# Attention memory term in 64 by 64 TensorE tiles, and the first raw weights in pieces on SyncE's queue

## Chip, cores and metric

The kernel runs on one core of one Trainium2 chip. The metric is the time of one execution in device microseconds, the median over several runs.

## What is computed

Three stages follow each other; each hands its output to the next.

```python
# attention, B=4, H=8, S=576, D=64
scores = q @ k^T / sqrt(D), causal mask, softmax        -> a
local  = a @ v
q_p    = phi(q)                                         # elu(q) + 1
mem    = (q_p @ M_prev) / (q_p @ z_prev + 1e-6)
x      = sigmoid(beta) * mem + (1 - sigmoid(beta)) * local
# feed-forward one: 2304 tokens, 512 -> 2048 -> 512
y      = softplus(x @ w_in) @ w_out
# feed-forward two: 512 -> 1536 -> 512
out    = ((y @ w_a) * (y @ w_b)) @ w_2
```

All inputs and outputs are float32.

## The kernel before

**Attention** works on 16 units, one for each batch and pair of heads (class `Unit`). A unit's q and k lie turned, 64 feature rows of one head in partitions 0 to 63 and those of the other in 64 to 127. `score` (L504) multiplies 64 rows by 128 columns at a time, the two heads beside each other in the two halves of the array's rows. `score_tail` (L531) does the last 64 tokens of both heads with all 128 rows. `memory` (L547) multiplies `ph`, which is phi(q), with `mz`, which holds M_prev and z_prev in 65 columns: for each of five blocks of 128 tokens and each head one float32 matmul with 64 rows and 128 columns of weights (`ph`) and 65 moved columns (`mz`). The trace shows each float32 matmul as two loads of weights and two matmuls. `turn`, `turn_tail` and `spread` (L589, L606, L607, L627) transpose, and `use` and `finish` (L619, L639, L645) multiply with v, 128 rows by 64 columns, into the two halves of the output's partitions.

**The reciprocal sums** of a unit travel through DRAM: DVE copies a transposed row (`rt`, L563), SP writes it to `rsd` (L565) and reads it back into all partitions as `rb` (L568). `finish` multiplies with `rb` on DVE (L635, L647).

**Feed-forward** stages multiply with seven products in place of eight (class `Seven`), each in three passes of rounded and rest parts (L850 for single blocks, L994 for the wide ones). Weights come as raw 64-bit words into two buffers `raw` of 8 KB per partition, and `decode` (L728 to L736) makes float32 of them with DVE and ACT, in halves (step 2) where `left_parts` calls it. The first two blocks of w_in are loaded by ACT's own DMA queue while attention still runs; every later one by SP's. `right_parts` (L775) loads x of a third of the tokens (`raw` from `xs`) for the same stage.

**The order** on all engines is made ahead of time by `Plan.order`: a planner gives every step a duration and a rank (the longest path behind it), plays the engines, and at each moment starts on SP, DVE, ACT and POOL the ready step with the highest rank; PE keeps written order within a stream and takes feed-forward matmuls only where attention has none ready. A DMA of SP takes its place on one modelled lane (`lane`) after the ones before it, and at most `LANES` of them are under way. The order is then fixed: on the chip each queue runs in it, and waits only for data.

Of the kernel before, what the change touches and what calls it, by code (L numbers as in the profile page):

```python
# [12 lines left out]
AF = mybir.ActivationFunctionType  # L13
# [16 lines left out]

FIRST, LAST = (0, 1), (6, 7)
START, CONST, WORDS = 6272, 1280, 55680
SWITCH, LANES = 190, 6


class Step:
# [16 lines left out]
class Plan:  # L53
# [153 lines left out]
    def order(self):  # L207
        steps = self.steps
        for s in steps:
            s.after, s.rank = [], 0  # L210
        for s in steps:
            for d in s.deps:
                steps[d].after.append(s.n)
        for s in reversed(steps):
            far = 0
            for a in s.after:
                t = steps[a]
                far = max(far, t.rank + (0 if t.eng == s.eng == "PE" else s.lag))
            s.rank = s.time + s.size + far
        for s in steps:  # L220
            s.left, s.ready, s.start = len(s.deps), 0.0, None
        engines = ("PE", "DVE", "ACT", "POOL", "SP")
        free = dict.fromkeys(engines, 0.0)
        soon, now = {e: [] for e in engines}, {e: [] for e in engines}
        for s in steps:
            if not s.left:
                heapq.heappush(soon[s.eng], (0.0, s.n))
        t, lane, done, mode, landed, held = 0.0, dict.fromkeys(engines, 0.0), 0, None, [], {"DVE": 0.0, "POOL": 0.0}
        port = None
        while done < len(steps):  # L230
            nxt = float("inf")
            moved = False
            for e in engines:
                while soon[e] and soon[e][0][0] <= t:
                    n = heapq.heappop(soon[e])[1]
                    s = steps[n]
                    heapq.heappush(now[e], ((s.stream, n) if e == "PE" else (-s.rank, n)))
                if free[e] > t:
                    nxt = min(nxt, free[e])
                    continue  # L240
                if e == "SP" and now[e] and len(landed) >= LANES and landed[-LANES] > t:
                    nxt = min(nxt, landed[-LANES])
                    continue
                if not now[e]:
                    if soon[e]:
                        nxt = min(nxt, soon[e][0][0])
                    continue
                s = steps[now[e][0][1]]
                if e in ("DVE", "ACT") and soon[e]:
                    u = max((steps[n] for r, n in soon[e] if r - t < min(0.25 * s.time, 150)), key=lambda u: u.rank, default=None)  # L250
                    if u and u.rank > s.rank + 3000:
                        nxt = min(nxt, u.ready)
                        continue
                if s.port and held[e] > t:
                    free_ = [x for x in now[e] if not steps[x[1]].port]
                    if not free_:
                        nxt = min(nxt, held[e])
                        continue
                    s = steps[min(free_)[1]]
                now[e].remove(next(x for x in now[e] if x[1] == s.n))  # L260
                heapq.heapify(now[e])
                s.start = t
                end = t + s.time
                if s.port:
                    held["POOL" if e == "DVE" else "DVE"] = end
                    if e == "DVE":
                        port = s.n
                    elif port is not None:
                        s.deps.add(port)
                if e == "PE":  # L270
                    if s.mode != mode:
                        end += SWITCH if not mode or s.mode[:2] != mode[:2] else SWITCH // 2 + 30 * (not s.mode[2])
                    mode = s.mode
                free[e] = end
                if s.size:
                    end = lane[e] = max(lane[e], end) + s.size
                    if e == "SP":
                        landed.append(end + s.lag)
                for a in s.after:
                    u = steps[a]  # L280
                    lag = 0 if u.eng == s.eng == "PE" else s.lag
                    u.ready = max(u.ready, end + lag)
                    u.left -= 1
                    if not u.left:
                        heapq.heappush(soon[u.eng], (u.ready, a))
                done += 1
                moved = True
                nxt = min(nxt, free[e])
            if not moved:
                t = nxt  # L290
        self.end = t
        return sorted(steps, key=lambda s: (s.start, s.n))
# [25 lines left out]
def tile_kernel(ctx: ExitStack, tc: tile.TileContext, qt, kt, vt, mz, be, w_in, w_out, w_a, w_b, w_2, out):  # L318
# [111 lines left out]
    both = (top, low)  # L430
# [23 lines left out]
    class Unit:  # L454
# [17 lines left out]
        def prep_k(self, first=False):  # L472
            kr, qr = self.kr, self.qr
            self.qh, self.ql, self.kh, self.kl = (take(n) for n in ("qh", "ql", "kh", "kl"))
            e = V if first else G
            for c, d in ((0, 256), (256, 640)) if first else ((0, 640),):
                k, q = slice(c, min(d, S)), slice(c, d)
                rnd(e, self.kh[:, k], kr[:, k])
                self.begun = {A.activation(out=self.qh[:, q], in_=qr[:, q], func=AF.Copy).n}
                sub(e, self.kl[:, k], kr[:, k], f(self.kh[:, k]))  # L480
                sub(e, self.ql[:, q], qr[:, q], f(self.qh[:, q]))

# [56 lines left out]
        def memory(self, k):  # L539
            p, ph, mz = self.p, self.ph, mzs[self.b % 2]  # L540
            self.mo = mo = blocks(take("mo"))
            nm = take("nm")
            banks = bank[:, k : k + 2]
            s = banks[:, :, 0:325].rearrange("p j (c e) -> p j c e", c=5)
            for c in range(5):
                for j, r in enumerate(both):
                    PE.matmul(  # L547
                        out=s[:, j, c], lhsT=ph[r, 128 * c : 128 * c + 128], rhs=mz[r, p], start=c == 0, stop=True, skip_group_check=True,
                    )
            by = lambda t: t.rearrange("p (j c) -> p j c", j=2)  # L550
            V.scalar_tensor_tensor(out=by(nm), in0=s[:, :, :, 64], scalar=1e-6, in1=by(self.rs), op0=ALU.add, op1=ALU.mult)
            V.reciprocal(out=nm, in_=nm)
            V.tensor_tensor(
                out=mo.rearrange("p c (j e) -> p j c e", j=2), in0=s[:, :, :, 0:64],
                in1=by(nm).unsqueeze(3).to_broadcast([128, 2, 5, 64]), op=ALU.mult,
            )
# [98 lines left out]
    order = [Unit(b, p) for b in range(B) for p in range(NP)]  # L655
# [66 lines left out]

    PASSES = ((0, 0), (0, 1), (1, 0))

    def decode(src, to, step=4, q=SP):

        raw = take("raw").bitcast(U32).rearrange("p (m c) -> p m c", c=2)
        q.dma_start(out=raw, in_=src).deps.update(order[1].begun if q is A else ())  # L728
        four = lambda t: t.rearrange("p (b n) -> p b n", b=4)
        for b in range(0, 4, step):  # L730
            low, high = (four(raw[:, :, i])[:, b : b + step] for i in range(2))
            V.tensor_scalar(out=low, in0=low, scalar1=29, scalar2=None, op0=ALU.logical_shift_right)
            V.scalar_tensor_tensor(out=low, in0=high, scalar=0x80000000, in1=low, op0=ALU.bitwise_and, op1=ALU.bitwise_or)  # L733
            A.activation(out=f(high), in_=f(high), func=AF.Identity, scale=REBIAS)  # L734
            V.tensor_scalar(out=f(high), in0=f(high), scalar1=MOST, scalar2=-MOST, op0=ALU.min, op1=ALU.max)
            V.scalar_tensor_tensor(  # L736
                out=to.bitcast(U32)[:, b : b + step], in0=high, scalar=3, in1=low, op0=ALU.logical_shift_left, op1=ALU.bitwise_or
            )
# [16 lines left out]
    def left_parts(src, at, e=V):  # L755

        w, d = (t.rearrange("p (n h m) -> p n h m", n=7, h=2) for t in twice("w", 3584, at))
        d = d[:, :, 1]
        decode(src, d[:, 0:4], 2, SP if e is V else A)
        left_sums(*(d[:, n] for n in range(7)), e)  # L760
        for n, m in ((0, 1), (1, 2), (4, 5), (2, 4), (5, 7)):
            rnd(A, w[:, n:m, 0], d[:, n:m])
            sub(e, w[:, n:m, 1], d[:, n:m], f(w[:, n:m, 0]))
        return lambda n, h, k: w[:, SLOT[n], h, 128 * k : 128 * k + 128]
# [443 lines left out]
```

## Time and profile before

| | us |
|---|---|
| runs | 938.68, 938.79, 940.41 |
| median | 938.79 |
| profiled execution | 940.39 |
| its span, first to last instruction | 938.6 |
| PE busy in it | 922.6 (98%) |
| DVE, ACT, POOL busy | 791.1 (84%), 566.8 (60%), 103.0 (11%) |
| mean granted TensorE clock | 0.998 |

The profile's times are those of the profiled execution. Attention takes about the first 194 us of the span. In the trace a matmul's shape on the array stands as rows*columns: 64*128 is half of the rows and all columns, 128*64 the reverse. PEld is the weight load that belongs to a matmul.

### The profile page before, as it was taken

Reading aid. Unit: us, or ns where it says so; the run is one execution under the profiler, and the core shown is the slowest. Engines: PE = TensorE matmul, PEld = TensorE weight load, DVE = VectorE, ACT = ScalarE, POOL = GpSimd, SP = SyncE. Lnnn points to the kernel's source line nnn. Section 1 sums busy time; section 2 is a strip of 40 time slices with the busy share of each in tenths; the row PEclk is TensorE's granted clock in tenths of the full one; section 3 lists DMA queues with packets and bytes.
Section 4 is the critical chain, followed back from the end, with each engine's and each line's share of the span. In section 5 each row is a group of like instructions: output and inputs, shape, how many; then the busy total and the mean of one; then the engine's idle time right before and its main releaser. Section 6 shows DMA issues by size and latency. Waiting matters only on the chain.

```text
span 938.6 us, 16918 instructions
## 1 busy us (share of the span) xinstructions
PE 922.6 (98%) x6204; PEld 890.1 (95%) x6204; DVE 791.1 (84%) x1503; ACT 566.8 (60%) x1124; POOL 103.0 (11%) x137
## 2 busy tenths in 40 slices
PE   7989999999999999999999999999999999999998
PEld 6878788899999999999999999999999999999998
DVE  7969989979998946998679999999997566998683
ACT  8968999757766756754446555544444334555452
POOL 6434588200000000000000000000000000000000
PEclk9999999999999999999999999999999999999999
DMA  6654564376988899482641444466654146672701
GB/s 185 193 162 131 169 186 130 99 232 215 312 292 293 267 329 370 172 299 73 202 135 34 134 157 159 159 226 208 224 188 144 43 160 192 245 234 74 225 32 50
DMA packets 81378, 172.10 MB, mean 183 GB/s; under 512 B 7936, under 2 KB 60560, under 8 KB 76048
## 3 DMA queue, kind: packets, MB, share of 16 engines
q1 hardware_dynamic: 80576, 168.61, 54.4%
q10 hardware_dynamic: 720, 2.43, 0.7%
q8 instruction: 48, 0.79, 0.3%
q14 instruction: 34, 0.28, 0.1%
HBM read 110.90 MB, written 60.10 MB: 182 GB/s over the span
## 4 chain that ended last, share of the span: by engine, by line
PE 86%; DVE 5%; ACT 3%; DMA 3%; issue 1%; POOL 1%; SPq 0%; DVEq 0%; POOLq 0%; ACTq 0%
PE bank L850 46%; PE bank L994 33%; DMA rb<-rsd 2%; PE bank L619 1%; PE bank L504 1%; PE bank L589 1%; PE bank L547 1%; DVE eTrue L514 1%; ACT eTrue L518 1%; PE bank L531 1%; ACT eFalse L518 1%; DMA kr<-kt 1%; PE bank L606 1%; PE bank L627 0%; ACT aT L595 0%
## 5 line engine op out<-in xcount | busy, mean ns | idle before, releaser
L340 DVE TENSOR_TENSOR s<-bank,s 128x384 f32<-128x384 f32 x216 | 117.2, 552 | 44.9 <-PE bank L850 38.9
L828 ACT ACTIVATE s<-bank 128x384 f32<-128x384 f32 x72 | 35.1, 487 | 73.2 <-PE bank L850 43.1
L337 DVE TENSOR_TENSOR t<-t,t 128x1536 f32<-128x1536 f32 (+1 forms) x48 | 74.5, 1552 | 0.4
L850 PE MATMUL bank<-x1h,w 128*128 128x384 f32 x240 | 71.0, 335 | 0.0
L850 PE MATMUL bank<-x6h,w 128*128 128x384 f32 x240 | 70.7, 335 | 0.3 <-ACT s L825 0.3
L850 PE MATMUL bank<-x5h,w 128*128 128x384 f32 x240 | 70.5, 334 | 0.0
L850 PE MATMUL bank<-x2h,w 128*128 128x384 f32 x240 | 70.5, 334 | 0.0
L850 PE MATMUL bank<-x3h,w 128*128 128x384 f32 x240 | 70.5, 334 | 0.0
L850 PE MATMUL bank<-x7h,w 128*128 128x384 f32 x240 | 70.5, 334 | 0.0
L850 PE MATMUL bank<-x4h,w 128*128 128x384 f32 x240 | 70.5, 334 | 0.0
L330 ACT ACTIVATE w<-wf 128x256 fp32r<-128x256 f32 (+1 forms) x100 | 50.0, 500 | 20.4 <-DVE w L337 16.4
L886 ACT ACTIVATE s<-s 128x384 f32<-128x384 f32 x72 | 37.2, 523 | 33.0 <-DVE s L340 32.9
L825 ACT ACTIVATE s<-bank 128x384 f32<-128x384 f32 x72 | 35.1, 487 | 35.8 <-PE bank L850 22.9
L330 ACT ACTIVATE gx2h<-t 128x768 fp32r<-128x768 f32 x37 | 31.4, 848 | 35.9 <-PE bank L994 32.7
L337 DVE TENSOR_TENSOR w<-wf,w 128x256 fp32r<-128x256 f32 (+1 forms) x90 | 47.2, 525 | 5.5 <-ACT w L330 4.9
L330 ACT ACTIVATE gx1h<-t 128x768 fp32r<-128x768 f32 x37 | 31.3, 846 | 33.4 <-PE bank L994 33.4
L734 ACT ACTIVATE raw<-raw 128x512 f32<-128x512 f32 (+1 forms) x54 | 42.6, 802 | 12.4 <-DVE raw L733 12.1
L330 ACT ACTIVATE gx0h<-t 128x768 fp32r<-128x768 f32 x37 | 31.3, 846 | 29.4 <-PE bank L994 28.5
L337 DVE TENSOR_TENSOR gx0l<-t,gx0h 128x768 fp32r<-128x768 f32 x37 | 35.3, 954 | 14.2 <-ACT gx0h L330 13.9
L518 ACT ACTIVATE eTrue<-eTrue,mn 128x384 f32<-128x384 f32 (+1 forms) x64 | 42.1, 660 | 8.2 <-DVE mn L514 8.0
L337 DVE TENSOR_TENSOR gx1l<-t,gx1h 128x768 fp32r<-128x768 f32 x37 | 35.3, 954 | 13.2 <-ACT gx1h L330 13.1
L831 ACT ACTIVATE s<-bank 128x384 f32<-128x384 f32 x72 | 35.1, 488 | 18.6 <-PE bank L850 14.6
(344 smaller groups left out, 3040.7 us busy)
## 6 DMA issues: line engine op xcount, KB each, us to landing
gs<-s SPq DMA_DIRECT2D x96, 192.0 KB
t<-gs SPq DMA_DIRECT2D x24, 768.0 KB
us<-s SPq DMA_DIRECT2D x72, 192.0 KB
t<-us SPq DMA_DIRECT2D x12, 768.0 KB
raw<-w_out SPq DMA_DIRECT2D x8, 1024.0 KB
raw<-w_in SPq DMA_DIRECT2D x6, 1024.0 KB
raw<-w_a SPq DMA_DIRECT2D x6, 1024.0 KB
raw<-w_b SPq DMA_DIRECT2D x6, 1024.0 KB
```

The lines of the kernel that those rows point to most:

```text
L330: A.activation(out=o, in_=i, func=AF.Copy)
L337: eng.tensor_tensor(out=o, in0=a, in1=b, op=ALU.subtract)
L340: eng.tensor_tensor(out=o, in0=a, in1=b, op=ALU.add)
L504: PE.matmul(out=s[:, j, at : at + L], lhsT=a[r, qc], rhs=b[r, 0:L], start=t == 0, stop=t == 2, skip_group_check=True,)
L518: A.activation(out=e, in_=e, func=AF.Exp, scale=-1.0, bias=mn[:, n : n + 1], accum_out=sm[:, n : n + 1])
L734: A.activation(out=f(high), in_=f(high), func=AF.Identity, scale=REBIAS)
L825: A.activation(out=self.s1, in_=bank["b"], func=AF.Copy)
L828: A.activation(out=self.s5, in_=bank["c"], func=AF.Copy)
L831: A.activation(out=self.s2, in_=bank["b"], func=AF.Copy)
L850: PE.matmul(out=o, lhsT=w(n, a, k), rhs=x[n][c][:, k], start=start and k == t == 0, stop=k == 1 and t == 2, skip_group_check=True,)
L886: A.activation(out=s, in_=s if bank is None else bank, func=AF.Softplus)
L994: PE.matmul(out=o, lhsT=self.w[n][a][:, u, 128 * m : 128 * m + 128], rhs=x[c][:, j], start=start and u == t == 0, stop=u == self.nu - 1 an ...
```

## The change

- `memory` cuts each matmul into two with 64 columns of weights, one for the upper and one for the lower half of the output's partitions. A unit has twenty matmuls of 64 rows by 64 columns in place of ten of 64 by 128; both write the same values to the same places. The four of a block lie in the four quarters of the array.
- `decode` loads raw words on SP's queue always. The first two blocks of w_in come in four pieces of 256 KB each instead of one of 1 MB on ACT's queue; later ones that `left_parts` decodes come in two pieces of 512 KB; those of `spill` stay whole.
- The planner holds back a large DMA of SP (over 300 ns in its model) while its modelled lane is more than 500 ns behind, so that a small one with a higher rank that becomes ready in the meantime goes first. This acts on all of the order.

```diff
-SWITCH, LANES = 190, 6
+SWITCH, LANES, AHEAD = 190, 6, 500
...
+                if e == "SP" and now[e] and steps[now[e][0][1]].size > 300 and lane[e] > t + AHEAD:
+                    nxt = min(nxt, lane[e] - AHEAD)
+                    continue
...
-                self.begun = {A.activation(out=self.qh[:, q], in_=qr[:, q], func=AF.Copy).n}
+                A.activation(out=self.qh[:, q], in_=qr[:, q], func=AF.Copy)
...
             for c in range(5):
-                for j, r in enumerate(both):
-                    PE.matmul(
-                        out=s[:, j, c], lhsT=ph[r, 128 * c : 128 * c + 128], rhs=mz[r, p], start=c == 0, stop=True, skip_group_check=True,
-                    )
+                for half in both:
+                    at = slice(128 * c + half.start, 128 * c + half.stop)
+                    for j, r in enumerate(both):
+                        PE.matmul(
+                            out=s[half, j, c], lhsT=ph[r, at], rhs=mz[r, p], start=c == 0, stop=True, skip_group_check=True,
+                        )
...
-    def decode(src, to, step=4, q=SP):
+    def decode(src, to, step=4, load=4):
...
-        q.dma_start(out=raw, in_=src).deps.update(order[1].begun if q is A else ())
+        for b in range(0, 1024, 256 * load):
+            m = slice(b, b + 256 * load)
+            SP.dma_start(out=raw[:, m], in_=src[:, m])
...
-        decode(src, d[:, 0:4], 2, SP if e is V else A)
+        decode(src, d[:, 0:4], 2, 2 if e is V else 1)
```

Lines move: L547 becomes L552, L728 becomes L735, and so on. The order that the planner makes differs at three places that the prediction speaks of.

First, the raw weights. Before, they stand in ACT's order behind the turns of the second unit (buffers `raw`, source `w_in`):

```order
L536 ACTIVATE eT_96,sm_123<-eT_96,mn_125 128x576
L595 ACTIVATE aT_112<-bank,og_60 128x256 x2
L728 DMA raw_62<-w_in 128x2048
L728 DMA raw_63<-w_in 128x2048
L486 ACTIVATE pos_78<-qr_67 128x640
```

Now they stand in SP's order among the loads of later units, ahead of the first unit's `rb`:

```order
L466 DMA kr_65<-kt 128x576
L735 DMA raw_62<-w_in 128x512 x3
L467 DMA qr_67<-qt 128x640
L466 DMA kr_64<-kt 128x576
L735 DMA raw_62<-w_in 128x512
L735 DMA raw_63<-w_in 128x512
L570 DMA rsd<-rt_104 9x128
L735 DMA raw_63<-w_in 128x512
L466 DMA kr_65<-kt 128x576
L735 DMA raw_63<-w_in 128x512 x2
L573 DMA rb_118<-rsd 64x576 x2
```

All eight pieces are issued before the first `rb`; three of them between `rsd` and `rb`.

Second, PE around the memory part of a unit, before:

```order
L504 MATMUL bank<-kl_74,qh_68 128x512 x2
L504 MATMUL bank<-kh_72,ql_70 128x512 x2
L547 MATMUL bank<-mz_102,ph_77 128x65 x10
L619 MATMUL bank<-aT_106,vr_97 64x512
L619 MATMUL bank<-aT_107,vr_97 64x512
```

and now:

```order
L507 MATMUL bank<-kl_74,qh_68 128x512 x2
L507 MATMUL bank<-kh_72,ql_70 128x512 x2
L552 MATMUL bank<-mz_102,ph_77 64x65 x20
L624 MATMUL bank<-aT_106,vr_97 64x512
L624 MATMUL bank<-aT_107,vr_97 64x512
```

The place is the same; PE's order is the same throughout but for a few feed-forward matmuls between the last units.

Third, SP where x of the first third of the tokens is loaded for feed-forward one (`raw` from `xs`), before:

```order
L565 DMA rsd<-rt_104 9x128
L652 DMA xs<-xx_121 128x384
L463 DMA kr_65<-kt 128x576
L775 DMA raw_62<-xs 128x1536
L568 DMA rb_118<-rsd 64x576 x2
L446 DMA mz_103<-mz 128x260
```

and now:

```order
L570 DMA rsd<-rt_104 9x128
L657 DMA xs<-xx_121 128x384
L657 DMA xs<-xx_121 128x192
L466 DMA kr_65<-kt 128x576
L573 DMA rb_118<-rsd 64x576 x2
L782 DMA raw_62<-xs 128x1536
L449 DMA mz_103<-mz 128x260
```

The load of 768 KB has moved from ahead of a unit's `rb` to behind it.

## Rows read from the trace of the kernel before

**Rows 1.** The page, part 1: busy time of the engines.

```profile
PE 922.6 (98%) x6204; PEld 890.1 (95%) x6204; DVE 791.1 (84%) x1503; ACT 566.8 (60%) x1124; POOL 103.0 (11%) x137
```

**Rows 2.** Windows, mostly unit by unit: length, PE, PEld, DVE, ACT, POOL busy, clock, DMA.

```profile
33.64:44.24 10.60, 10.60 (x123) 8.99 (x121) 10.02 (x30) 9.78 (x28) 4.38 (x6) 1.00 0.67 186
44.24:60.40 16.16, 12.57 (x123) 10.60 (x120) 9.26 (x34) 9.05 (x25) 4.73 (x7) 0.89 0.71 229
60.40:71.72 11.32, 10.76 (x122) 9.00 (x120) 11.10 (x33) 10.11 (x28) 3.97 (x5) 1.00 0.43 125
...
104.90:116.99 12.09, 11.85 (x136) 9.97 (x134) 11.53 (x39) 10.87 (x29) 5.97 (x8) 1.00 0.39 125
...
138.93:149.52 10.59, 10.59 (x123) 8.98 (x120) 10.17 (x32) 10.59 (x30) 9.31 (x11) 1.00 0.47 141
...
200.00:400.00 200.00, 200.00 (x1156) 200.00 (x1155) 170.87 (x288) 136.81 (x258) 0.00 (x0) 1.00 0.83 281
```

**Rows 3.** Waits of PE: us in total, times, longest.

```profile
PE bank L589 <- DVE rt L563: 3.6, 1, 3.6
```

**Rows 4.** Timeline of ACT's DMA queue, and a window from 40 us.

```profile
41.34 0.82 ACTq L728 DMA_DIRECT2D raw<-w_in  x2
...
40.00:48.00 8.00, 8.00 (x85) 6.49 (x85) 7.62 (x25) 7.18 (x21) 3.14 (x4) 1.00 0.97 330
```

**Rows 5.** Chain that ended last, 43 us, and DVE's timeline behind it.

```profile
43.43 9.33 DMA rb<-rsd
...
52.78 0.69 DVE L635 TENSOR_TENSOR xx<-bank,rb 128x512 f32<-128x512 f32 x1 [1.47 <-DMA rb<-rsd]
```

**Rows 6.** PE timeline, transposes of two units, and a window's clock in the second.

```profile
40.33 0.97 PE L589 MATMUL bank<-ident,eTrue 128*128 128x128 f32 x7
...
54.92 1.39 PE L589 MATMUL bank<-ident,eTrue 128*128 128x128 f32 x7
...
54.76:58.16 3.40, 3.40 (x18) 3.07 (x18) 2.31 (x5) 2.07 (x5) 3.01 (x4) 0.57 0.20 73
```

**Rows 7.** PE timeline around the memory part of two units: start, length.

```profile
138.93 1.34 PE L547 MATMUL bank<-mz,ph 64*128 64x65 f32 x20
140.20 2.37 PE L619 MATMUL bank<-aT,vr 128*64 128x512 f32 x16
...
179.98 0.60 PE L627 MATMUL bank<-ident,mo 128*128 128x128 f32 x4
180.51 1.33 PE L547 MATMUL bank<-mz,ph 64*128 64x65 f32 x20
```

**Rows 8.** PEld timeline in narrow windows: weight loads on one tile and on two.

```profile
22.39 0.29 PEld L547 LDWEIGHTS bank<-mz,ph 64*128 64x128 f32 x2 [0.43 <-DVE ph L489]
22.86 0.19 PEld L547 LDWEIGHTS bank<-mz,ph 64*128 64x128 f32 x2 [0.18 <-DVE mn L514]
...
140.20 0.14 PEld L619 LDWEIGHTS bank<-aT,vr 128*64 128x64 f32 x2
140.20 0.20 PEld L619 LDWEIGHTS bank<-aT,vr 128*64 128x64 f32 x4
```

**Rows 9.** PE timeline of sixteen small matmuls in two column tiles.

```profile
142.40 0.63 PE L639 MATMUL bank<-aT,vr 128*64 128x64 f32 x16
```

**Rows 10.** SP's queue, DVE's first use of `rb`, and a window.

```profile
20.18 0.35 SPq L565 DMA_DIRECT2D rsd<-rt  x1
20.84 0.35 SPq L463 DMA_DIRECT2D kr<-kt  x1
21.45 1.10 SPq L568 DMA_DIRECT2D rb<-rsd  x2
...
27.24 0.22 DVE L647 TENSOR_TENSOR xx<-bank,rb 64x64 f32<-64x64 f32 x1 [0.23 <-PE bank L645]
...
24.00:26.00 2.00, 2.00 (x14) 0.93 (x15) 1.97 (x7) 1.94 (x5) 1.01 (x1) 1.00 0.30 89
```

**Rows 11.** SP's queue at 93 us, and the chain behind it.

```profile
93.32 0.87 SPq L775 DMA_DIRECT2D raw<-xs  x1
...
94.79 6.82 DMA rb<-rsd
```

## The prediction

> **What bounds the kernel now.** I read the busy times first: PE is busy 98% of the span [rows 1]. Then windows: from 200 us on PE has no gap (200.00 of 200.00) and DVE is below it [rows 2]. The change leaves the matmuls of feed-forward as they are, so a gain has to come from attention, the first 194 us, and reaches the end because the dense part only starts earlier. In attention I cut the windows from one unit's memory part to the next [rows 2]. The shortest is 10.6 us, with PE without a gap. One is 16.16 us, 5.56 more. Between others DVE or ACT is as full as PE: DVE 11.10 of 11.32, ACT 10.59 of 10.59.
>
> The long unit holds the only large wait of PE after the start, 3.6 us, for DVE's copy of the sums [rows 3]. DVE was late because its product with `rb` waited for a DMA: the chain shows `rb` under way for 9.33 us, and DVE starting right after it [rows 5]. Just before, ACT's queue had issued both 1 MB loads of raw weights, and the DMA engines were 97% busy from 40 to 48 us [rows 4]: a transfer of 288 KB shared them with 2 MB. The stall costs twice. After it the granted clock is 0.57 in a window, so most of it ran at 1.2 GHz after PE had stood still, and seven transposes took 1.39 us instead of 0.97 [rows 6].
>
> **Term A, the raw weights.** Their eight pieces are issued among the loads of later units, before the first `rb`, and have landed long before the unit that stalled. What goes is the excess of that window, 16.16 − 10.60 = 5.56 us [rows 2]. What is late next: the first `rb`. Three pieces (768 KB) now stand in SP's queue between `rsd` at 20.18 and `rb` at 21.45 [rows 10]. At 330 GB/s, the rate of the window at 40 us [rows 4], they take 0.79 us each, 2.4 us together; their issues (0.35 us each as the `kr` load) fall into the wait for `rsd`. Until now that `rb` had landed by about 25 us, since the window behind it shows the DMA engines 30% busy, and DVE used it at 27.24, where it waited for PE and not for `rb` [rows 10]: about 2.2 us of slack. With the memory part shorter everything before it comes a little earlier, so I count 0.6 us of new wait. A is 5.56 − 0.6 = −5.0 us. Its bounds: −5.6 with no new wait, −4.0 if 1.5 us of it comes back. The pieces let decoding of w_in start one half at a time; the same instructions on DVE and ACT as before, so no term.
>
> **Term B, a load that moved behind `rb`.** At 93.32 SP issued a load of x, 768 KB, just ahead of a unit's `rb`, which then took 6.82 us [rows 11]. The window after it is 12.09 us [rows 2], 1.49 over the shortest; but DVE is busy 11.53 of these, so not all of that was waiting. Behind `rb` the load disturbs less: −0.7 us, between 0 and −1.5. The other large loads of SP that the planner's new rule moves lie under a PE without gaps [rows 2], which covers them as long as each lands before its use; without that cover each microsecond that one is late would be one of the end. I cost them at nothing.
>
> **Term C, the memory part.** It runs from 138.93 to 140.20, 1.27 us, of which twenty records take 1.34 − 0.27 = 1.07 from the first start to the last, a pair every 0.11 us [rows 7] (0.27 is one record's length). What sets that pace is the weight load. Where only one head's tile was ready, two loads of 128 columns took 0.29 us, each 0.18 long: one starts 0.11 after the other, though the other tile was idle. Where both are ready, two loads start within 0.01 us [rows 8]. So a load of 128 columns holds its tile for 0.11 us, and two row tiles load at the same time. In column tiles two loads of 64 columns start together, and the next two 0.06 us later (0.20 − 0.14) [rows 8]: half the columns, half the time, again at the same time in both. Sixteen small matmuls there take 0.63 us, 0.22 of it the last one's length, so a pair comes every 0.41 / 7 = 0.058 us [rows 9]. If four quarters work as independently as two halves do, a block's four records come every 0.058 us; forty records are ten such groups, 0.58 us in place of ten pairs at 0.11, 1.12 us: −0.54.
>
> What is added: before, score and memory had the same array shape, and the first memory record followed without a gap. Now the shape changes once more. A change of shape is seen at 180.51: the last transpose started at 179.98 + 0.60 − 0.27 = 180.31, the memory part 0.20 later, where the pace is 0.11 [rows 7]: 0.09, and the first load, 0.06 for 64 columns, is no longer hidden. So +0.15 for each unit that follows scores, fifteen, and none for the last. C on PE alone is 15 × (−0.54 + 0.15) − 0.54 = −6.4 us. No row shows four quarters at work, so the bounds are −6.4 and, if records come no closer than 0.029 us on average as in the fastest row [rows 9], 40 × 0.029 = 1.17, +0.05 + 0.15 = +0.20 for each of fifteen, +3.0. I take the independent quarters, for the two sets of rows (row tiles, column tiles) both show it.
>
> But not all of −6.4 reaches the end: ACT is busy all of a 10.6 us window and DVE up to 98% of another [rows 2], and then PE only waits earlier. I take half, −3.2 us.
>
> A page of the Trainium skill speaks against this step: TensorEngine Tiling (Array Packing), section Instruction Overhead, says that each matmul has about 60 cycles of overhead, so that one shouldn't tile where a dimension is small already. By it (25 ns at 2.4 GHz, an estimate from that page) forty records would need 1.0 us and C would be about zero. The same skill's TensorE: Matmul & The Clock Gate, Part 3: Packing small matmuls, has tiles starting some 4 ns apart, with which the 0.01 us between two loads agrees; no run here has an average pace below 29 ns.
>
> **Sum.** −5.0 − 0.7 − 3.2 = −8.9 us. Against the profiled execution, 940.39 us (span 938.6 and 1.8 around it), that gives 931.5. This execution lies 1.6 above the median of the runs, 938.79, so I take the sum from the median: **929.9 us**. About 0.2% (1.9 us) is what a measurement can tell from no change here.
>
> **Rivals.** *Quarters that don't run beside each other.* C is then +3.0 and A and B stay: 938.79 − 5.0 − 0.7 + 3.0 = 936.1. For it: only two tiles at a time appear in any row. Against it: both kinds of halves are independent. The page on tiling in the Trainium skill, named above, would put it at 933.1, with C at zero. *The other engines swallow C.* DVE and ACT set the pace, and only A and B are left: 933.1. For it: their full windows [rows 2]; against it: the shortest windows have PE without a gap, and their neighbours of 10.6 us show DVE at 10.02 and 10.17.
>
> *Slower: the stall moves instead of going.* All raw weights now share one queue with `rb`. If the eight pieces still lay in front of the first `rb` whole, 2 MB at 330 GB/s, it would land 6.4 us later, 4.2 past its slack; with the slow clock after such a gap (16.16 − 10.60 − 3.6 = 2.0 us beyond the wait itself [rows 2, 3]) that is 6.2 us at 27 us of the span, for the 5.6 that went. Together with memory parts that gain nothing, +3.0, the time is 938.79 + 0.6 + 3.0 = 942.4. It decides from a landing more than 2.2 us late on. Against it: five of the eight pieces stand before `rsd` in SP's order, and at 0.79 us each they need 4 us. *The change does not do what it says*, another load takes the place of the raw ones in that window, or the new order starves feed-forward by as much as attention gains: no change, 938.8.
>
> **Chances.** The forecast 0.55; quarters not beside each other 0.19; other engines swallow C 0.11; no change 0.07; slower 0.08. Faster by over 0.2% takes the first three, less a little for their poor ends: 0.83. Within 0.2%: 0.09. Slower: 0.08. The range reaches down to all of A, most of B and C whole, 938.79 − 5.6 − 1.3 − 6.4 = 925.5, and up past the first rival with A at 5.0 and B at 0, 936.8, to **925.5 to 937.0**.
>
> **What would show it.** A: no ACT queue row for raw weights, no 9 us `rb` near 43 us, no 3.6 us wait of PE behind `rt`, a clock of 1.00 there, and that unit at about 10.5 us. A wait of DVE for `rb` near 27 us would measure the 0.6. B: the unit near 105 us below 11.5. C: the memory row with 40 records, 0.8 us long instead of 1.34, and four loads starting within 0.03 us; 1.2 us or more would mean the first rival. If the row is short but units stay at 10.6 us with ACT or DVE full, it is the second. Dense feed-forward should start at 185 instead of 194 us. A gap of PE after 200 us would make the prediction wrong, and so would `rb` of the first unit landing after 28 us.

## The result, and the profile after

The changed kernel takes 927.5 us (median of four runs, 927.4 to 927.63) where the kernel before takes 939.44 (four runs, 938.68 to 940.41). The ratio is 0.9872, with a 95% interval from 0.9855 to 0.9889: 11.9 us faster. The forecast was 929.9 us, 8.9 below the 938.79 that the kernel before had from its first three runs; it lay 2.4 us too high, and its range holds the result.

The profiled execution took 927.4 us, with a span of 925.5. The page, part 1, of the changed kernel (answers to [rows 1]):

```profile
PE 913.2 (99%) x6524; PEld 877.4 (95%) x6524; DVE 793.0 (86%) x1503; ACT 566.6 (61%) x1124; POOL 103.2 (11%) x137
```

PE has 320 records more and is busy 9.4 us less. DVE and ACT do what they did.

Windows of the changed kernel, from one unit's memory part to the next, then most of attention, then feed-forward (length, PE, PEld, DVE, ACT, POOL busy, clock, DMA share, GB/s; compare [rows 2]):

```profile
33.58:44.19 10.61, 10.54 (x141) 8.24 (x141) 9.91 (x33) 10.10 (x28) 4.47 (x6) 1.00 0.47 147
44.19:54.97 10.78, 10.60 (x142) 8.47 (x141) 10.64 (x37) 9.71 (x29) 4.92 (x7) 1.00 0.63 190
...
96.86:107.03 10.17, 10.17 (x142) 8.27 (x141) 9.51 (x32) 10.17 (x30) 8.18 (x9) 1.00 0.62 185
149.33:159.48 10.15, 10.15 (x142) 8.26 (x140) 9.45 (x32) 10.15 (x30) 9.11 (x10) 1.00 0.27 84
33.00:165.00 132.00, 130.21 (x1780) 103.91 (x1777) 124.79 (x408) 123.07 (x343) 77.85 (x92) 1.00 0.51 154
200.00:400.00 200.00, 199.78 (x1153) 199.46 (x1152) 175.28 (x289) 135.71 (x248) 0.00 (x0) 1.00 0.85 283
```

The unit of 16.16 us is now 10.78, with the clock at 1.00. The best units have fallen from 10.6 to 10.15, and in them PE and ACT are both busy all the time. Feed-forward is as full as before but for 0.2 us in 200.

Waits of PE in the changed kernel (us in total, times, longest; compare [rows 3]):

```profile
PE bank L507 <- DVE kh L335: 5.0, 1, 5.0
PE bank L611 <- DVE aT L602: 1.8, 6, 0.5
...
PE bank L612 <- DVE xx L652: 0.3, 1, 0.3
```

The first is the start of the kernel, as before. The wait for `rt` of 3.6 us is gone. Two more rows of the kernel before belong beside these; the first of them lies in the unit that starts at 93.60:

```profile
PE bank L607 <- DVE xx L647: 1.3, 1, 1.3
PE bank L606 <- DVE aT L597: 1.0, 3, 0.6
```

That wait for `xx` is gone too, and one of 0.3 us stands elsewhere. The short waits for DVE's `aT` have grown, from 1.0 us in three places to 1.8 in six.

PE timeline around one memory part of the changed kernel (start, length of the group; compare [rows 7]), and the loads of its first block:

```profile
33.16 0.49 PE L507 MATMUL bank<-kh,ql 64*128 64x512 f32 x2
33.58 0.81 PE L552 MATMUL bank<-mz,ph 64*64 64x65 f32 x40
34.32 2.38 PE L624 MATMUL bank<-aT,vr 128*64 128x512 f32 x16
```

```profile
33.58 0.15 PEld L552 LDWEIGHTS bank<-mz,ph 64*64 64x64 f32 x4 [0.36 <-DVE rs L584]
```

The part takes 34.32 − 33.58 = 0.74 us where it took 1.27. Its first four loads end 0.15 us after the first starts; one alone is 0.13 long, so they start within about 0.02 us: four quarters work beside each other.

All of the gain comes in attention. From one memory part to the next the fifteen stretches take, in us, worked out from the starts of these groups in each trace:

```
before    8.23 11.25 10.60 16.16 11.32 11.20 10.68 12.37 11.03 10.87 11.07 10.59 10.89 10.67 9.43 | last starts at 180.51
changed   8.20 11.20 10.61 10.78 10.40 10.63 10.22 10.65 10.17 10.46 10.87 10.62 10.35 10.15 8.08 | last starts at 167.57
```

The last memory part starts 12.9 us earlier and the span ends 13.1 earlier. Of the 12.9, the stalled unit gives 5.4, the unit of 12.37 gives 1.7, and the others give 5.8 in small pieces. The chain's last piece, the dense feed-forward, starts at:

```profile
179.56 20.50 PE bank L857 x117
```

In the kernel before it starts at 193.69, 14.1 us later. The end gains about 1 us less than that, because 13 of the feed-forward matmuls, some 0.17 us each, had by then already run between those of attention, and now only 7 have.

### The profile page after: what moved, and what is told of

Its sections match the earlier page's. It is cut to its first block, busy times and chain, and to the rows that moved or that the text cites. A ratio compares the mean times of both kernels' runs of the same rounds, so it can differ in the third digit from the quotient of the medians.

```text
span 925.5 us, 17542 instructions
## 1 busy us (share of the span) xinstructions
PE 913.2 (99%) x6524; PEld 877.4 (95%) x6524; DVE 793.0 (86%) x1503; ACT 566.6 (61%) x1124; POOL 103.2 (11%) x137
## 4 chain that ended last, share of the span: by engine, by line
PE 89%; DVE 6%; ACT 2%; DMA 1%; issue 1%; POOL 0%; SPq 0%; DVEq 0%; ACTq 0%
PE bank L857 47%; PE bank L1001 33%; PE bank L507 2%; PE bank L624 2%; DVE eTrue L517 1%; PE bank L594 1%; PE bank L534 1%; DMA kr<-kt 1%; PE bank L611 1%; PE bank L552 1%; DVE eT L535 1%; PE bank L632 1%; DVE xx L640 1%; DVE ph L492 1%; DVE aT L602 1%
## 5 line engine op out<-in xcount | busy, mean ns | idle before, releaser
L340 DVE TENSOR_TENSOR gx1l<-t,gx1h 128x768 fp32r<-128x768 f32 x37 | 35.3, 954 | 13.0 <-ACT gx1h L333 12.9
L333 ACT ACTIVATE gx3h<-t 128x768 fp32r<-128x768 f32 x36 | 30.5, 846 | 26.1 <-PE bank L1001 26.1
```

The lines of the kernel that those rows point to most:

```text
L333: A.activation(out=o, in_=i, func=AF.Copy)
L340: eng.tensor_tensor(out=o, in0=a, in1=b, op=ALU.subtract)
```

## Experiments

The runs of the kernel before that stood beside the experiments had medians of 940.09, 940.09 and 940.5 us. Times are medians. Where nothing else is said, an edit is to the changed kernel, and the planner then makes the order anew. The changed kernel was not run again beside them, so a difference to its 927.5 is one between separate sets of runs. That they compare is seen in the traces: from the last memory part to the end of the span all fourteen take between 756.9 and 759.4 us.

**1. The old matmuls in the new order.** The memory part goes back to ten matmuls of 64 by 128, but the planner is told the durations of the new ones, so that every engine's order is that of the changed kernel.

```diff
+                if n == 65:
+                    s.time, s.mode = 2 * 2 * max(n / 1.2 + 3, 64 * 0.42 * 2) / 4, (64, 64, False, True)
...
-                for half in both:
-                    at = slice(128 * c + half.start, 128 * c + half.stop)
-                    for j, r in enumerate(both):
-                        PE.matmul(out=s[half, j, c], lhsT=ph[r, at], ...)
+                for j, r in enumerate(both):
+                    PE.matmul(out=s[:, j, c], lhsT=ph[r, 128 * c : 128 * c + 128], ...)
```

> The changed kernel with the memory part back in ten matmuls of 64 by 128, while the planner is told the durations of the new ones, so that the order on every engine stays that of the changed kernel. What is left of the change is the raw weights on SyncE's queue and the held-back loads. Theory (the memory part pays about half of what PE saves, the rest of the gain is the stall): the memory block is 1.27 us again instead of 0.74 in each of 16 units, and the time is 3 to 5 us above the changed kernel's 927.5, so 930.5 to 932.5. Rival 1 (ACT and DVE set the pace of a unit, the smaller tiles pay nothing): within 1 us of 927.5. Rival 2 (PE is the limit in every unit): 0.53 x 15 = 8 us above, 935.5.

930.42 us (929.67 to 930.68), ratio 0.9894 [0.9878, 0.991]. So in this order the tiles are worth 930.42 − 927.5 = 2.9 us, just below what the theory gave, and most of the gain stands without them. The intervals of the two ratios overlap, but the runs do not, and in the traces the last memory part starts 2.8 us later. PE timeline, the window over most of attention, and the chain's shares by line in it:

```profile
33.81 0.47 PE L509 MATMUL bank<-kh,ql 64*128 64x512 f32 x2
34.04 1.35 PE L552 MATMUL bank<-mz,ph 64*128 64x65 f32 x20
35.32 1.94 PE L624 MATMUL bank<-aT,vr 128*64 128x512 f32 x10
```

```profile
33.00:165.00 132.00, 131.84 (x1487) 111.07 (x1487) 123.68 (x405) 123.43 (x336) 76.96 (x90) 1.00 0.50 152
```

```profile
by line: PE bank L624 20.6%; PE bank L509 19.2%; PE bank L594 18.2%; PE bank L552 10.7%; PE bank L536 8.2%; PE bank L644 4.8%; PE bank L611 4.7%; PE bank L632 4.0%; DVE eTrue L519 1.7%; PE bank L612 1.0%; PE bank L650 1.0%; PE bank L567 0.9
```

With the old matmuls this order keeps PE full, 131.84 of 132 us, and PE makes the chain almost alone. With the new ones PE drops to 130.21: part of what the tiles save turns into short waits. Since the order is the same, the starts of the matmuls in the two traces can be compared one by one: the changed kernel gains 6.6 us at its sixteen memory parts and loses 3.8 of them again at the transposes of L594 and L611. Weight loads of the second of these wait for DVE in the same window, in the changed kernel and here:

```profile
PEld bank L611 <- DVE aT L602: 3.2, 7, 0.8
```

```profile
PEld bank L611 <- DVE aT L602: 0.8, 3, 0.4
```

**2. Two tiles at a time.** The same forty small records, the same order, but the upper halves of all blocks first, so that neighbours in the order use two of the four quarters.

```diff
-            for c in range(5):
-                for half in both:
+            for half in both:
+                for c in range(5):
```

> The changed kernel with the same twenty memory matmuls in another order: first the five blocks of the upper half, then the five of the lower, so that neighbours in the order use two of the four quarters and the other two only after ten matmuls. Theory (matmuls start in order, each tile takes its own every 0.058 us, so only different tiles next to each other run at once): a pair every 0.058 us, forty records in about 1.2 us and the block about 1.3 us long, and the time 2.5 to 4 us above 927.5. Rival (the engine finds free quarters by itself, or the pace comes from smaller loads alone): the block stays near 0.8 us and the time within 0.5 us of 927.5.

929.65 us (929.46 to 929.86), 0.9891 [0.9867, 0.9916]. PE timeline:

```profile
33.91 1.21 PE L552 MATMUL bank<-mz,ph 64*64 64x65 f32 x40
35.05 2.15 PE L624 MATMUL bank<-aT,vr 128*64 128x512 f32 x12
```

The part takes 1.14 us, as expected, though the time fell 0.35 us under the expected 930 at best. Between this kernel and the changed one only the issue order of forty records differs: 1.14 against 0.74, sixteen times 0.40 = 6.4 us on PE, of which 929.65 − 927.5 = 2.15 reach the end, a third. So 2.15 of the 2.9 us that the tiles are worth come from four at once; the 0.8 between this kernel and experiment 1 are what smaller tiles bring two at a time.

**3. Same instructions as in 1, planned for the old matmuls.** The old loop as in 1, without the lines for the planner.

> The changed kernel with the memory part in ten matmuls of 64 by 128 and the order planned for it: raw weights in pieces on SyncE's queue and held-back loads are left of the change. It asks whether the order made for the short memory part is itself what gains. Theory (it is not; the raw weights' new place gains 9 us by itself): within 1 us of the run that kept the changed kernel's order, 929.5 to 931.5. Rival (the order does it): 933 or more.

934.36 us (934.14 to 935.31), 0.9937 [0.9917, 0.9957]. This is 3.9 us above experiment 1, with the same matmuls and loads and, but for some feed-forward matmuls, the same order on PE. Only the order on the other engines and SP differs. Window and chain:

```profile
33.00:165.00 132.00, 129.61 (x1437) 107.23 (x1434) 121.53 (x389) 121.39 (x329) 80.16 (x94) 1.00 0.51 159
```

```profile
by line: PE bank L507 12.9%; PE bank L622 12.2%; PE bank L592 10.5%; DVE eTrue L517 6.8%; PE bank L550 6.3%; PE bank L534 4.5%; issue 4.5%; DMA rb<-rsd 4.4%; DVE eT L535 4.4%; PE bank L609 4.1%; DVE ph L492 3.7%; PE bank L630 3.3%; PE bank 
```

Here the chain goes through DVE far more often, and through a transfer of `rb` (4.4% of it), which experiment 1 does not show. That does not mark the slower order by itself: the chain of the changed kernel holds 3.7 us of `rb` in this window, that of experiment 5 even 10.6%. The rival, that the order brings what the tiles seem to, is shown for 3.9 us.

**4. New matmuls, an order planned for slow ones.** The planner is told the old duration for the new tiles, and no change of array shape.

```diff
+                if n == 65:
+                    s.time, s.mode = max(n / 1.2 + 3, 128 * 0.42 * 2) / 2, (64, 128, False, True)
```

> The changed kernel's matmuls, while the planner is told the durations of the old ones, 64 by 128 (about 0.5 us more per unit and no change of array shape). With the run of old tiles in the changed kernel's order this closes a square of two tilings and two ways of planning. Theory (the order that is planned for a lighter PE is better by itself by about 4 us, the tiles by about 3): 930.5 to 932.5. Rival (the tiles only pay in an order planned for them): 933.5 or more. Rival 2 (order is worth nothing here, the earlier run was scatter): within 1 us of 927.5.

935.84 us (935.77 to 936.76), 0.9949 [0.9932, 0.9966].

```profile
33.00:165.00 132.00, 124.21 (x1663) 98.03 (x1659) 121.02 (x384) 121.49 (x329) 80.98 (x95) 1.00 0.51 156
```

PE is free 7.8 of 132 us and the end is no earlier than in experiment 3. The two orders are close but not the same on DVE, ACT and SP, so this suggests, and does not show, that in an order that waits for DVE and DMA faster matmuls only wait longer.

**5. New matmuls, an order planned for even faster ones.** The planner is told a quarter of the duration, and no change of array shape.

```diff
+                if n == 65:
+                    s.time, s.mode = s.time / 4, (64, 128, False, True)
```

> The changed kernel, while the planner is told a quarter of the memory part's duration and no change of array shape, some 0.6 us less per unit than it takes on the chip. Theory (planning for a lighter PE than there is puts DVE's and ACT's late work ahead and gains more): 925 to 927. Rival (orders scatter by some microseconds whatever the planner is told, and the changed kernel's is a good draw): 928 to 932.

926.59 us (926.54 to 926.64), 0.9849 [0.983, 0.9868], the fastest kernel of the study: 0.9 us below the changed one, whose four runs all lie above these. The ratios' intervals overlap.

```profile
33.00:165.00 132.00, 131.03 (x1791) 105.02 (x1790) 124.59 (x412) 123.84 (x338) 74.42 (x89) 1.00 0.50 154
```

PE keeps 131.03 of 132 us where it keeps 130.21 in the changed kernel: more of what the tiles save seems to arrive, in an order of its own.

**6. The kernel before in another order.** To learn what an order alone is worth, one planner constant of the kernel before.

```diff
-SWITCH, LANES = 190, 6
+SWITCH, LANES = 200, 6
```

> The kernel before with one number of the planner's model moved by 10 ns (the cost of a change of array shape, 190 to 200) and nothing else: the same instructions in a slightly different order. It measures by how much the time scatters with the order alone. Theory (a small change of the order is worth less than 1.5 us): 938.5 to 941.5. Rival (scatter of 2 us and more, which would put the 4 us of the order in doubt): outside of that.

940.46 us (937.46 to 942.18), 0.9997 [0.9982, 1.0012]. This change of order is worth nothing in the median. In the profiled execution, with a span of 935.4 us, the stalled unit took 13.73 us instead of 16.16: the stall has no fixed size.

**7. The raw move alone.** The changed kernel with the old memory loop, and without the hold-back.

```diff
-SWITCH, LANES, AHEAD = 190, 6, 500
+SWITCH, LANES, AHEAD = 190, 6, 1.0e9
```

> The kernel before with the raw weights in pieces on SyncE's queue and nothing else: no held-back loads, memory part in matmuls of 64 by 128. Theory (this part alone makes most of the gain: it removes the stall at 44 us and lets DVE decode w_in over more units, so that the units behind are no longer full): no unit over 11.6 us, 930 to 932. Rival (only the stall goes, the units from 60 to 117 us stay at 11.2 us on average): 934 to 935.5.

936.04 us (935.56 to 936.15), 0.9955 [0.9943, 0.9968]: −4.05, less than my theory's and 0.5 us above the rival's bracket. The unit of 16.16 us is gone (11.07 in its place). But units of 12.16 and 12.13 us start at about 22 and 111 us.

**8. The hold-back alone.** Only the planner's new rule, in the kernel before.

```diff
+                if e == "SP" and now[e] and steps[now[e][0][1]].size > 300 and lane[e] > t + AHEAD:
+                    nxt = min(nxt, lane[e] - AHEAD)
+                    continue
```

> The kernel before with only the planner's new rule: a large load of SyncE is held back while the modelled queue is over 500 ns behind. Raw weights stay on ACT's queue, the memory part in matmuls of 64 by 128. Theory: the stall near 44 us stays; the x load no longer stands ahead of rb near 93 us, and the two units there lose 1 to 2.5 us: 937 to 939. Rival 1 (the rule does nothing): equal to before within 0.5 us. Rival 2 (the rule alone brings most of the gain): below 934.

941.09 us (940.38 to 942.4), 1.0011 [0.9999, 1.0023]: nothing. The units at 93 us went from 12.37 and 11.03 to 11.07 and 10.99, which is term B's place and, at 1.3 us, inside its bounds; others gave it back. The stall stays, as PE's wait shows:

```profile
PE bank L592 <- DVE rt L566: 4.7, 4, 3.9
```

**9. The tiles alone.** Only the new memory loop, in the kernel before (the loop as the change has it).

> The kernel before with the memory part in twenty matmuls of 64 by 64 and nothing else; the order is planned anew. Theory: the 5 us stall near 44 to 53 us of the span stays (rb under way for some 9 us, PE waiting 3 us or more), and the units gain about half of PE's 0.53 us each: 3 to 5 us below before, 934.5 to 936.5. Rival 1 (other engines set the pace): within 1 us of before, 938.5 to 940. Rival 2 (PE is the limit): 6 to 8 us below, 931.5 to 933.5.

932.65 us (932.25 to 934.23), 0.9922 [0.9904, 0.994]: −7.4, more than the 3 to 5 of my theory and within the rival's bracket. The stall is untouched: from the memory part at 53.11 to the next at 69.24 the unit takes 16.13 us. A window that starts a little earlier shows its clock:

```profile
51.88:68.01 16.13, 11.95 (x144) 9.32 (x144) 10.17 (x31) 9.36 (x26) 4.77 (x6) 0.89 0.73 253
```

The other units became shorter, three of them 10.12 to 10.17 us. The order was planned anew here too, so this −7.4 holds both effects, tiles and order.

**10. The pieces on ACT's queue.** All of the change, but the first raw weights in their pieces on the queue they were on, behind the second unit's `qh` as before.

```diff
-                A.activation(out=self.qh[:, q], in_=qr[:, q], func=AF.Copy)
+                self.begun = {A.activation(out=self.qh[:, q], in_=qr[:, q], func=AF.Copy).n}
...
-            SP.dma_start(out=raw[:, m], in_=src[:, m])
+            if load == 1:
+                A.dma_start(out=raw[:, m], in_=src[:, m]).deps.update(order[1].begun)
+            else:
+                SP.dma_start(out=raw[:, m], in_=src[:, m])
```

> The changed kernel with the first raw weights still in four pieces each, but on ACT's queue and behind the same ACT instruction as in the kernel before. Theory (the stall came from 2 MB sharing the DMA engines with rb at that moment): a long rb (over 6 us) and a wait of PE or DVE of 2 us or more near 45 us come back, and the time is 4 to 6 us above 927.5, 931.5 to 933.5. Rival (the size of one transfer mattered, and pieces let rb through): no such wait, within 1 us of 927.5.

929.89 us (929.16 to 931.61), 0.9892 [0.9869, 0.9914]: 2.4 us above the changed kernel, less than the 4 to 6 of the theory. ACT's queue issues the pieces between 50.85 and 74.04 us, and the units that start at 53.83 and 65.27 take 11.44 and 12.50. In each of them one half of `rb` lands 7.0 us after its issue, and PE waits 1.1 and 1.3 us for `rt`. PE's waits for `rt` in the whole run, and DVE's for `rb` in the second of these units:

```profile
PE bank L594 <- DVE rt L568: 2.6, 3, 1.3
```

```profile
DVE xx L640 <- DMA rb<-rsd: 0.4, 1, 0.4
```

So with the late loads on ACT's queue the chain of the stall comes back, but in two units, and smaller. The order is another one too, and not all of the 2.4 us need be this: a longer wait of DVE for `rb`, 3.6 us, stands at 183 us in the last unit, far from the pieces.

**11. Without the hold-back.** `AHEAD` as in 7, all else as in the change.

> The changed kernel without the planner's new rule on large loads. Theory (the rule alone brought nothing, and brings nothing here): 927 to 929, no wait of DVE for rb over 1 us. Rival (without it the raw pieces or an x load stand ahead of rb): a wait of DVE for rb of 2 us or more near 27 us or near 90 us, and 930 or more.

931.51 us (930.93 to 934.26), 0.9917 [0.9888, 0.9946]: 4.0 us above the changed kernel. Of these, 1.2 stand in one unit, 12.43 in place of 11.20, where PE waits for the product with the first `rb`. SP's queue, DVE around that product and PE's waits, without the hold-back:

```profile
20.26 0.36 SPq L570 DMA_DIRECT2D rsd<-rt  x1
...
24.52 0.33 SPq L467 DMA_DIRECT2D qr<-qt  x1
24.94 2.19 SPq L573 DMA_DIRECT2D rb<-rsd  x2
```

```profile
30.51 0.69 DVE L614 TENSOR_TENSOR aT<-bank,og 128x512 f32<-128x512 f32 x1
31.12 0.68 DVE L640 TENSOR_TENSOR xx<-bank,rb 128x512 f32<-128x512 f32 x1
```

```profile
PE bank L612 <- DVE xx L652: 3.5, 4, 1.6
```

And with it, in the changed kernel:

```profile
20.18 0.36 SPq L570 DMA_DIRECT2D rsd<-rt  x1
...
21.63 0.90 SPq L735 DMA_DIRECT2D raw<-w_in  x2
22.64 1.10 SPq L573 DMA_DIRECT2D rb<-rsd  x2
24.43 0.34 SPq L467 DMA_DIRECT2D qr<-qt  x1
```

```profile
29.59 0.67 DVE L640 TENSOR_TENSOR xx<-bank,rb 128x512 f32<-128x512 f32 x1
```

Without the rule `rb` stands behind the load of `qr` in SP's order, where SP waits 2.3 us until ACT has read the buffer that `qr` is to fill, and is issued 2.3 us later; DVE's fixed order has the product behind more turns, and it starts 1.53 us later. No engine is seen to wait for `rb` itself: the lateness is built into the order.

**12. Raw blocks whole on SP's queue.** The first two blocks in one piece of 1 MB each.

```diff
-        decode(src, d[:, 0:4], 2, 2 if e is V else 1)
+        decode(src, d[:, 0:4], 2, 2 if e is V else 4)
```

> The changed kernel with the first two blocks of raw weights whole, 1 MB each, on SyncE's queue; the order is planned anew. It tells the queue and the place from the pieces. Theory (what counts is that the loads are early and out of the way of rb; whole ones can still be held back to the right moment): no unit over 12 us, 927.5 to 930. Rival (1 MB ahead of a unit's rb stops DVE as before): a wait of DVE for rb of 2 us or more and 931 or more.

931.6 us (931.22 to 932.47), 0.9904 [0.9884, 0.9923]. The second unit takes 16.00 us in place of 11.20: the stall has moved to the first `rb`. SP's queue, DVE, PE's wait and a window behind it:

```profile
26.28 0.38 SPq L472 DMA_DIRECT2D vr<-vt  x1
26.75 1.11 SPq L573 DMA_DIRECT2D rb<-rsd  x2
```

```profile
31.81 0.41 DVE L739 TENSOR_SCALAR raw<-raw 128x512 uint32<-128x512 uint32 x1
32.15 0.68 DVE L640 TENSOR_TENSOR xx<-bank,rb 128x512 f32<-128x512 f32 x1
```

```profile
PE bank L612 <- DVE xx L652: 3.2, 2, 2.9
```

```profile
34.00:37.00 3.00, 3.00 (x23) 2.67 (x23) 1.69 (x5) 1.90 (x5) 0.00 (x0) 0.50 0.63 201
```

Now `rb` stands behind `vr` as well and is issued at 26.75; DVE decodes ahead of the product, PE waits 2.9 us, and then the granted clock is 0.50, the lower of its two levels. With the order that comes with it, the whole loads cost 4.1 us: the pieces are a part of the gain.

**The parts together.** "Raw" is the pieces on SP, "hold" the hold-back:

| kernel | raw | hold | new tiles | us |
|---|---|---|---|---|
| before (beside 1 to 5, and 7 to 12) | | | | 940.1 to 940.5 |
| 7 | x | | | 936.0 |
| 8 | | x | | 941.1 |
| 9 | | | x | 932.7 |
| 3 | x | x | | 934.4 |
| 11 | x | | x | 931.5 |
| 10, pieces on ACT | | x | x | 929.9 |
| changed | x | x | x | 927.5 |

The parts don't add up: the raw move is worth 4.1 us by itself, 6.7 beside the hold-back, 1.1 beside the tiles. Each of these steps also makes a new order. Only experiments 1 and 2 against the changed kernel hold the order fixed.

## Why the prediction was right, and which step of it failed

I go by one path through the runs: before, 7, 3, 1, changed, from 940.1 to 927.5, 12.6 us. By another path the parts have other sizes, as the table shows.

**Term A** (forecast −5.0, measured alone −4.05) was right in its mechanism. The ACT queue's raw rows are gone, so is the `rb` of 9 us (3.9 now) and the wait of 3.6 us, and the unit is 10.78 us, 5.4 shorter, where 5.56 were counted. Experiment 10 brings a part of the stall back. Of the new wait of 0.6 us behind the first `rb`, half came, and not as I had named it: DVE doesn't wait for `rb`, but PE waits 0.3 us at L612 for the product with it. The sharing of the DMA engines that I counted on is seen: of the issues of `rb` from 20 to 32 us, the one at 23.14 took longest to land,

```profile
DMA to landing us min/median/max: 4.2/5.2/6.1
```

and landed at 29.3, past the 28 us that I had named as a sign against me. That sign was wrong: DVE's order has other steps until 29.59, and the unit takes 11.20 us, where it took 11.25. What I had not seen is a second cause, the place in the order. In experiments 11 and 12 `rb` stands behind loads of `qr` and `vr`, and the product behind other steps on DVE, and PE's wait at L612 grows to 1.6 and 2.9 us.

**Term B** (−0.7) had the place right and the size too small. My window from 104.90 does not start at a memory part: these start at 93.60, 105.97 and 116.99. So the unit with the `rb` of 6.82 us took 12.37, 1.77 over the shortest, with PE waiting 1.3 us in it for the product (L607). The next one took 11.03 already, so my sign for B, a unit below 11.5 near 105 us, could not have failed. The hold-back shortens these two units by 1.3 us (experiment 8), and on top of the raw move it is worth 936.0 − 934.4 = 1.7; by itself it gains nothing.

**Term C** (−3.2) was right: 2.9 with the order fixed. The pace that I took from the row tiles and column tiles, one group of four every 0.058 us, gave 0.58 from the first start to the last; the part of 0.81 less the last record's 0.22 is 0.59. The change of shape, counted at 0.15, costs 0.42 − 0.23 = 0.19 in the rows of the changed kernel and of experiment 1, where the two heads are somewhat apart, and 0.32 − 0.23 = 0.09 in most other units, where they are in step. On PE alone the forecast was 6.4 us, and the traces of experiment 1 show 6.6. The share that reaches the end, taken as a half without a row for it, is 2.9 of 6.6 by experiment 1 and a third of what experiment 2 adds; the rest is lost at transposes that wait for DVE and ACT, as the rows of experiment 1 show for L611.

Of the rivals, quarters that don't work beside each other are out (0.74 us for the part, and 1.14 in experiment 2, where only two can). By the Trainium skill's TensorEngine Tiling (Array Packing), section Instruction Overhead, forty records would have needed 1.0 us, an estimate from that page; the trace disagrees, with 0.74 to the start of the next part. The Trainium skill's TensorE: Matmul & The Clock Gate, Part 3: Packing small matmuls, with starts some 4 ns apart, is the nearer of the two: four loads start within 0.02 us. That the other engines swallow C holds for more than half of it in experiment 1, for two thirds in experiment 2, and, as far as two close orders can be compared, for all in experiment 4.

**The step that failed** is the one that put the new order at nothing: "The other large loads of SP that the planner's new rule moves lie under a PE without gaps", "I cost them at nothing", and "the same instructions on DVE and ACT as before, so no term". I had read the order on PE and at three places, and treated the rest as the same work. From experiment 3 to experiment 1 nothing changes but the order that DVE, ACT, POOL and SP have for the same instructions, and the place of some feed-forward matmuls, and that is 3.9 us, more than the tiles themselves. It is almost all of what the sum lacks: −4.05 − 1.7 − 3.9 − 2.9 = −12.6 against −5.0 − 0.7 − 3.2 = −8.9. With it, dense feed-forward starts at 179.6 and not at 185.

That the result lies in the range is in part luck. The gain was 11.9 us where 8.9 were counted; the time came nearer than the gain, because the fourth run of the kernel before raised its median by 0.65. A was 0.95 smaller along this path and B 1.0 larger, which cancels by chance, and the term that was missing was as large as any but A.

What an order does is shown at one place only, the first `rb`, and that is not where experiments 3 and 1 differ: in their traces 13 of the fifteen stretches are longer in experiment 3, by 1.1 us at most, and the one with the first `rb` is not among them. I varied what the planner is told of the new tiles: with the old duration they end at 935.8 us, with the new one at 927.5, with a quarter of it at 926.6. A planner that thinks PE faster seems to put the work that feeds PE earlier; that reading was not tested step by step, and which steps carry the 3.9 us stays open.

## What to carry to other kernels

Where an order is computed from durations, a new duration is an edit of every engine's order: cost it as a term of its own, and test a change of a matmul with the old order held fixed. Small matmuls with two narrow dimensions pay when those issued one after another lie in different quarters of the array; what they save reaches the end only as far as DVE and ACT are ahead. A small transfer that a later product needs should be issued ahead of loads that wait for a free buffer, not only ahead of large ones.

## What the runs showed that I had not expected

- **Issue order decides how many tiles work at once.** The same forty records take 0.74 us with the four quarters in turn and 1.14 us with two quarters at a time (experiment 2), though nothing but the order of issue differs.
- **The kernel with the stall scatters.** The kernel before lies between 937.95 and 943.29 us over the runs beside the experiments, 5.3 us apart; the changed one within 0.23, experiment 5 within 0.10. The stalled unit was 16.16 us long in one profile and 13.73 in that of experiment 6. Whether the scatter comes from the stall stays open: experiment 7, without it, lies within 0.6 us in nine runs, but experiment 11, also without it, 3.3 apart in four.
- **A planner's wrong duration can be the better one.** Told a quarter of the matmuls' time and no change of shape, it made the fastest order of the study, 926.59 us.
